# Layer 1 takes three of its blocks from SBUF, a third buffer for the norm's parts, the FFN's weights in one tile

## Chip, cores and metric

One core of a Trainium2 chip (trn2) runs the kernel. The time is that of one execution on the device, in microseconds (us). Of several executions the median is given. The engines of the core are TensorE (PE, matrix products), VectorE (DVE), ScalarE (ACT), GpSimd (POOL) and SyncE (SP, which here only issues transfers). PSUM is the memory that PE writes its sums to, SBUF the on-chip memory of all engines, DRAM the memory outside.

## What is computed

A sequence of 2048 rows with 512 features goes twice (two layers, same weights) through a state-space convolution and a gated feed-forward network, each behind a layer norm and with a residual:

```python
x = A_u                                   # [1, 2048, 512] float32
for layer in (0, 1):
    # A: causal convolution along the rows, per feature, with a kernel K of 2048 taps
    #    K[d, l] = Re(sum_n C[d, n] * exp(dt[d] * A[d, n] * l) * dt[d] * B[d, n]),  N = 128
    #    by FFT of length 4096, plus u * Dskip
    x = x + _A_ref(_layernorm(x), A_re, A_im, B_re, B_im, C_re, C_im, log_dt, Dskip)
    # B: (silu(x @ w_gate) * (x @ w_up)) @ w_down,   512 -> 1376 -> 512
    x = x + _B_ref(_layernorm(x), w_gate, w_up, w_down)
```

## The kernel before

**Blocks.** The rows are cut into four blocks of 512 (`T`). The convolution is done block by block with transforms of 1024 points: block b needs its own spectrum and those of the blocks ahead of it, each times the spectrum of a piece of K. A block is named layer.block here. Layer 1 of a block needs layer 0 of that block and of those ahead, so the order is a free choice within that: `SEQ` is 0.0, 0.1, 0.2, 1.0, 0.3, 1.1, 1.2, 1.3. The first 300 us, the front, compute K from A, B, C (`gen_tiles` makes the factors, 64 features to a chunk, eight chunks; products L509 and L510), its spectra, and split the weights of the network into a high and a low f16 part. That part's order on SP is written out by hand; elsewhere a scheduler of the language fixes each engine's order ahead of the run, from a simulated timeline and from priorities (`tc.high_priority(offset=BOOST)` lifts what is inside it). At run time every engine takes its instructions strictly in that order.

**One block of the convolution.** `inputs` (its loop prints below) loads 512 rows into the tile n, norms them (`norm_x`: twelve activations on ACT; the results of the first eight, the statistics, go to a scratch tile "junk", L223 and L225), and transforms them (`forward`: z L267, products L277 into pf, evictions such as L278). `ssm_half` does one half of the features (256): the products of spectra with vector instructions on DVE (L812, L815, 128 x 1024 each), per half four quarters with b + 1 terms; the parts w and uu are loaded from DRAM (L808, L810). Then the inverse transform (`inverse`: yl L776 on ACT, products L784 on PE into pi), and `result` adds pi to the block's residual rows xt (L232). The residual rows are the tile xs[i % 3], where i is the place of the block in `SEQ`: xs[0] and xs[1] are the halves of one tile xg, xs[2] is xf. `load_x(xt, layer, b)` fills xt ahead of `result`: for layer 0 from the input, for layer 1 from `xdr`, a DRAM tile to which each block of layer 0 is stored at the end of its network (L957, four stores of 256 KB). The tile n is loaded from the same place (L238, 1 MB), so a block of layer 1 costs two loads of 1 MB.

**One block of the network.** `ffn` works on two halves of 256 rows. `ffn_norm` norms xt: statistics on ACT (L223, L225; their results are thrown into the tile nn2), then for each of two row tiles the normed rows into nn2[:, 0] (L883), the high f16 part into half of nn2[:, 1] (L884), the low part into the other half (L885, DVE), and two DMA transposes (L887) into nh and nlo, which lie in a tile called mix. All row tiles use the same two buffers, so L884 of the next one may write only after the transpose of the one ahead has read. Gate and up products (L930, L931, L933: high x high, high x low, low x high, 256 columns) go through two PSUM buffers pgu in groups of 48; each group is followed by Silu on ACT (L936), the product on DVE (L937, both into sg), and the high and low parts hh (L938, ACT) and hl (L939, DVE). 1376 features are ten full groups of 128 and a rest of 96, which `remainder` does with the rows as the stationary side: 48 products of 96 columns in each half (L899 to L901), then L907 to L909 and four DMA transposes (L913). The down products (L946 to L948, 512 columns) end in py, which L953 adds to xt; then the store.

In the emission the convolution of the next block stands ahead of the network of this block, so that PE's products of the network run while DVE works on the next block's spectra:

```python
    for i, lb in enumerate(SEQ):
        if i + 1 < len(SEQ):
            take(ssm(*SEQ[i + 1]) if i else block1, 100)
        if i == 0:
            take(pscale, 100)
        ffn(*lb, ready if i == 0 else None)
```

## Time and profile before

| | |
|---|---|
| three runs | 1089.46, 1092.52, 1093.47 us; median 1092.52 |
| the profiled execution | 1091.58 us; from the first to the last instruction 1089.4 us |
| mean granted clock of PE | 0.986 |
| busy: PE, DVE, ACT, POOL | 1026.5 us (94%), 969.3 (89%), 547.4 (50%), 109.6 (10%) |
| moved by DMA | 149.23 MB, mean 137 GB/s |
| loads n from xdr | 4 of 1024 KB, 6.4 us from issue to landing |
| ACT from 417 us on, waiting at L223 for n | 16.1 us for xdr, 6.5 for the input |

How to read the rows: a group of instructions stands as line, engine, operation, out<-in with tile names, partitions x elements and type, x count; behind the first bar its busy us and the mean ns of one, behind the second the engine's idle time just ahead of them and what ended most of it. A row that begins with a time is a single instruction or a run of alike ones: start in us, length in us, engine, line, and in brackets the idle time ahead of it and the instruction or transfer that ended it. "PEld" is PE's loading of the stationary side, "SPq" SP's sequencer. A table by stages has one row for each stretch A:B.

### The profile page before, as it was taken

Reading aid. Unit: us, or ns where it says so; the run is one execution under the profiler, and the core shown is the slowest. Engines: PE = TensorE matmul, PEld = TensorE weight load, DVE = VectorE, ACT = ScalarE, POOL = GpSimd, SP = SyncE. Lnnn points to the kernel's source line nnn. Section 1 sums busy time; section 2 is a strip of 40 time slices with the busy share of each in tenths; the row PEclk is TensorE's granted clock in tenths of the full one; section 3 lists DMA queues with packets and bytes.
Section 4 is the critical chain, followed back from the end, with each engine's and each line's share of the span. In section 5 each row is a group of like instructions: output and inputs, shape, how many; then the busy total and the mean of one; then the engine's idle time right before and its main releaser. Section 6 shows DMA issues by size and latency. Waiting matters only on the chain.

```text
span 1089.4 us, 22811 instructions
## 1 busy us (share of the span) xinstructions
PE 1026.5 (94%) x9302; PEld 810.9 (74%) x9302; DVE 969.3 (89%) x1405; ACT 547.4 (50%) x1093; POOL 109.6 (10%) x163
## 2 busy tenths in 40 slices
PE   1989999998779999999999999999999999999998
PEld 1868888887677777686779676786867687686775
DVE  8999999998999999999999989999998999993221
ACT  6989998953367162466462253533425432134211
POOL 1112222220002010012010001201100000000000
PEclk9989999998989999999999999999999999999999
DMA  5366777768765356342444553443545245312000
GB/s 212 108 180 167 173 166 179 187 181 272 234 182 172 120 145 215 105 141 68 131 117 133 158 160 130 119 136 100 166 126 180 59 127 147 109 61 63 2 25 20
DMA packets 125003, 149.23 MB, mean 137 GB/s; under 512 B 50897, under 2 KB 75985, under 8 KB 124130
## 3 DMA queue, kind: packets, MB, share of 16 engines
q1 hardware_dynamic: 112994, 122.27, 36.8%
q0 software_dynamic: 11904, 25.50, 10.0%
q8 instruction: 73, 1.20, 0.5%
q14 instruction: 32, 0.26, 0.1%
HBM read 97.66 MB, written 33.82 MB: 121 GB/s over the span
## 4 chain that ended last, share of the span: by engine, by line
PE 27%; DVE 27%; issue 11%; DMA 5%; ACT 3%; POOL 1%; SPq 0%; DVEq 0%; POOLq 0%; ACTq 0%
PE pgu L930 5%; PE pgu L931 5%; PE pgu L933 5%; DVE t L812 4%; DVE yk L815 4%; PE py L948 3%; PE py L946 3%; PE py L947 3%; DVE yk L812 3%; PE pi L784 2%; DVE sg L937 2%; DVE hl L939 2%; DMA n<-xdr 1%; DVE yl L232 1%; DMA mix<-nn 1%
## 5 line engine op out<-in xcount | busy, mean ns | idle before, releaser
L930 PE MATMUL pgu<-mix,wsl 128*128 128x256 f16 x1280 | 298.6, 273 | 5.4 <-DVE sg L937 2.1
L931 PE MATMUL pgu<-mix,wsl 128*128 128x256 f16 x1280 | 298.4, 273 | 0.0
L933 PE MATMUL pgu<-mix,wsl 128*128 128x256 f16 x1280 | 194.8, 273 | 0.0
L931 PEld LDWEIGHTS <-wsl 128*128 128x128 f16 x1280 | 125.2, 98 | 22.5 <-issue 6.7
L933 PEld LDWEIGHTS <-wsl 128*128 128x128 f16 x1280 | 125.2, 98 | 18.4 <-issue 3.8
L930 PEld LDWEIGHTS <-wsl 128*128 128x128 f16 x1280 | 125.2, 98 | 16.4 <-issue 1.2
L946 PE MATMUL py<-wsl,hh 128*128 128x512 f16 (+1 forms) x352 | 134.2, 381 | 0.1
L948 PE MATMUL py<-wsl,hl 128*128 128x512 f16 (+1 forms) x352 | 133.5, 381 | 0.1
L947 PE MATMUL py<-wsl,hh 128*128 128x512 f16 x320 | 121.8, 381 | 0.0
L815 DVE TENSOR_TENSOR yk<-yk,t 128x1024 f32<-128x1024 f32 x96 | 116.9, 1218 | 0.5
L812 DVE TENSOR_TENSOR t<-uu,w 128x1024 f32<-128x1024 f32 x96 | 117.0, 1218 | 0.3
L938 ACT ACTIVATE hh<-sg 128x512 f16<-128x512 f32 x80 | 50.1, 627 | 114.0 <-DVE sg L937 114.0
L544 PE MATMUL pw<-kt,ek 128*128 128x256 f32 (+1 forms) x384 | 93.2, 381 | 0.0
L937 DVE SCALAR_TENSOR_TENSOR sg<-pgu,sc,sg 128x512 f32<-128x512 f32 x80 | 59.6, 745 | 37.7 <-ACT sg L936 37.6
L936 ACT ACTIVATE sg<-pgu,sc 128x512 f32<-128x512 f32 x80 | 54.2, 678 | 70.7 <-PE pgu L933 66.9
L544 PEld LDWEIGHTS pw<-kt,ek 128*128 128x128 f32 x384 | 74.8, 199 | 8.8
L939 DVE TENSOR_TENSOR hl<-sg,hh 128x512 f16<-128x512 f32 x80 | 54.8, 685 | 15.3 <-ACT hh L938 15.3
L227 POOL TENSOR_TENSOR rs<-mv,mhalf 128x2 f32<-128x2 f32 (+1 forms) x21 | 33.6, 1598 | 336.3 <-ACT mv L226 296.3
L509 PE MATMUL pk<-re,g 128*32 128x64 f32 x1024 | 65.0, 317 | 2.2 <-DMA g<-g 1.9
L948 PEld LDWEIGHTS <-hl 128*128 128x128 f16 (+1 forms) x352 | 34.4, 98 | 39.2 <-issue 0.8
L947 PEld LDWEIGHTS <-hh 128*128 128x128 f16 (+1 forms) x352 | 34.6, 98 | 38.4 <-issue 0.8
L510 PE MATMUL pk<-im,g 128*32 128x64 f32 x1024 | 63.1, 301 | 0.0
(265 smaller groups left out, 2010.1 us busy)
## 6 DMA issues: line engine op xcount, KB each, us to landing
uu<-udr SPq DMA_DIRECT2D x96, 256.0 KB, 3.0
w<-wdr SPq DMA_DIRECT2D x96, 256.0 KB, 2.8
g<-g POOLq DMA_DIRECT2D x6, 1024.0 KB, 9.2
udr<-fu POOLq DMA_DIRECT2D x22, 256.0 KB, 2.7
udr<-u SPq DMA_DIRECT2D x16, 256.0 KB, 3.3
n<-xdr SPq DMA_DIRECT2D x4, 1024.0 KB, 6.4
kdr<-ks SPq DMA_DIRECT2D x6, 512.0 KB, 2.9
kt<-kdr SPq DMA_DIRECT2D x24, 128.0 KB, 3.0
```

Of the source, the lines that this page charges most:

```text
L509: PE.matmul(o, lhsT=g[:, 0, :, d], rhs=re[:, 0:64, d], start=True, stop=False, tile_position=(0, 32 * grp))
L544: PE.matmul(pw[:, i], lhsT=e, rhs=kt[:, :, c + 4 * k0:4 * k1:4, :].rearrange("p g k d -> p k g d"), start=c == 0, stop=c == 3)
L812: V.tensor_tensor(t, uu.unsqueeze(2).to_broadcast([P, NQ, 2, 2, DC]), w.unsqueeze(3).to_broadcast([P, NQ, 2, 2, DC]), OP.mult)
L815: V.tensor_tensor(yk, yk, t, OP.add)
L930: PE.matmul(o, lhsT=wgu(wi, k, 0)[:, fs], rhs=nh[:, k], start=k == 0, stop=False)
L931: PE.matmul(o, lhsT=wgu(wi, k, 1)[:, fs], rhs=nh[:, k], start=False, stop=False)
L933: PE.matmul(o, lhsT=wgu(wi, k, 0)[:, fs], rhs=nlo[:, k], start=False, stop=k == 3)
L937: V.scalar_tensor_tensor(sg, pgu[:, 1], sc6[:, 4:5], sg, OP.mult, OP.mult)
L939: V.tensor_tensor(hl[:, f0:f0 + 2], sg, hh[:, f0:f0 + 2], OP.subtract)
L946: PE.matmul(py[r], lhsT=hh[:n, f, rc], rhs=wd(f, 0)[:n], start=f == 0, stop=False)
L947: PE.matmul(py[r], lhsT=hh[:n, f, rc], rhs=wd(f, 1)[:n], start=False, stop=False)
L948: PE.matmul(py[r], lhsT=hl[:n, f, rc], rhs=wd(f, 0)[:n], start=False, stop=f == FT - 1)
```

## The change

- **Blocks.** A table `HOME` says which buffer a block has: xs[0] for 0.0, 1.0 and 1.2, xs[1] for 0.1 and 1.1, xs[2] for 0.2, 0.3 and 1.3. So 1.0, 1.1 and 1.3 find their residual rows where layer 0 left them. For these blocks neither n nor xt is loaded; `norm_x` takes its rows from xs and writes n. Block 1.2 (`MOVED`) still goes through DRAM, in a tile `xdr` of one block, and of layer 0 only 0.2 is stored.
- **The network's norm.** The parts of a row tile take the next two of a cycle of three f16 buffers: the two halves of nn2[:, 1] and a new tile nt3. The statistics' scratch results go to nn2[:, 0] alone.
- **Weights.** The four tiles W0 to W3, in which first the factors of K and later the split weights lie, and the small tile wx become one tile `wall`; gate and up columns of one k lie at a fixed distance, so that one access covers both. `remainder` does gate and up in one product of 192 columns: 24 products in each half.

```diff
 SEQ = ((0, 0), (0, 1), (0, 2), (1, 0), (0, 3), (1, 1), (1, 2), (1, 3))
+HOME = (0, 1, 2, 0, 2, 1, 0, 2)
+MOVED = 2
...
     wmax = sb.tile([P, 2], BF16, name="wmax")
-    wx = sb.tile([P, D], F16, name="wx")
+    wall = sb.tile([P, 4, 65 * DC], F32, name="wall")
+    wflat = wall.rearrange("p t a -> p (t a)").bitcast(F16)
+    wcols = wflat[:, :16 * F].rearrange("p (w u f) -> p w u f", w=2, u=8)
     ident = sb.tile([P, P], F32, name="ident")
...
     udr = [dram.tile([NB - 1, 2, 4, P, NQ, 2, DC], F32, name=f"udr{i}") for i in range(NL)]
-    xdr = dram.tile([NB, 4, P, D], F32, name="xdr")
+    xdr = dram.tile([4, P, D], F32, name="xdr")
     kdr = dram.tile([2, 4, 32, 4, 256], F32, name="kdr")
...
+    def moved(layer, b):
+        return layer == 0 or b == MOVED
+
     def load_x(xt, layer, b):
         if layer == 0:
             nc.sync.dma_start(xt, x[0, b * T:(b + 1) * T, :].rearrange("(p c) d -> p c d", p=P))
         else:
-            nc.sync.dma_start(xt, xdr[b].rearrange("c p d -> p c d"))
+            nc.sync.dma_start(xt, xdr.rearrange("c p d -> p c d"))
...
-    def norm_x(n):
-        rs, nb = row_stats(n, 4, 1.0, "stats", lambda r: tl([P, D], "junk", "t1", BF16))
+    def norm_x(n, xt):
+        rs, nb = row_stats(xt, 4, 1.0, "stats", lambda r: tl([P, D], "junk", "t1", BF16))
         for c in range(4):
-            A.activation(n[:, c], n[:, c], AF.Identity, scale=rs[:, c:c + 1], bias=nb[:, c:c + 1])
+            A.activation(n[:, c], xt[:, c], AF.Identity, scale=rs[:, c:c + 1], bias=nb[:, c:c + 1])
...
     def gen_tiles(ch):
-        re = tl([P, 65, DC], "re", f"W{2 * (ch % 2)}")
-        im = tl([P, 65, DC], "im", f"W{2 * (ch % 2) + 1}")
+        re, im = (wall[:, 2 * (ch % 2) + i].rearrange("p (a d) -> p a d", d=DC) for i in range(2))
         mu = tl([P, 32, DC], "mu", "n")
...
     def wgu(wi, kc, lo, n=1):
-        u = 8 * wi + 4 * lo + kc
-        v = wsl[u // 6].rearrange("p (u f) -> p u f", u=6)
-        return v[:, u % 6] if n == 1 else v[:, u % 6:u % 6 + n]
+        u = 4 * lo + kc
+        return wcols[:, wi, u] if n == 1 else wcols[:, wi, u:u + n]
 
     def wd(fc, lo):
         r = 2 * fc + lo
-        if r < 5:
-            return wsl[2][:, 4 * F + r * D:4 * F + (r + 1) * D]
-        return wsl[3][:, (r - 5) * D:(r - 4) * D] if r < 21 else wx
+        return wflat[:, 16 * F + r * D:16 * F + (r + 1) * D]
...
             n = tl([P, 4, D], "n", "n")
-            load_x(n, layer, b)
-            norm_x(n)
+            xt = n if moved(layer, b) else xs[HOME[SEQ.index((layer, b))]]
+            if xt is n:
+                load_x(n, layer, b)
+            norm_x(n, xt)
             if (layer, b) == SEQ[HALF]:
...
-        xt = xs[SEQ.index((layer, b)) % 3]
+        xt = xs[HOME[SEQ.index((layer, b))]]
         ys = []
...
                 a_, b_, c_, d_ = ys
-                if h == 0 and not first:
+                if h == 0 and not first and moved(layer, b):
                     load_x(xt, layer, b)
...
         rows = TB // P
-        xt = xs[SEQ.index((layer, b)) % 3][:, s * rows:(s + 1) * rows]
+        xt = xs[HOME[SEQ.index((layer, b))]][:, s * rows:(s + 1) * rows]
         nh, nlo = nhl2[:, s % 2, 0], nhl2[:, s % 2, 1]
         with tc.high_priority(offset=BOOST):
-            rs, nb = row_stats(xt, rows, 256.0, "stats2", lambda r: nn2[:, r])
-            nt = nn2[:, 1].bitcast(F16).rearrange("p (i k) -> p i k", i=2)
+            rs, nb = row_stats(xt, rows, 256.0, "stats2", lambda r: nn2[:, 0])
             for r in range(rows):
                 A.activation(nn2[:, 0], xt[:, r], AF.Identity, scale=rs[:, r:r + 1], bias=nb[:, r:r + 1])
-                A.activation(nt[:, 0], nn2[:, 0], AF.Copy)
-                V.tensor_tensor(nt[:, 1], nn2[:, 0], nt[:, 0], OP.subtract)
+                nt = [next(parts) for _ in range(2)]
+                A.activation(nt[0], nn2[:, 0], AF.Copy)
+                V.tensor_tensor(nt[1], nn2[:, 0], nt[0], OP.subtract)
                 for i, o in enumerate((nh, nlo)):
-                    nc.sync.dma_start_transpose(o[:, :, r * P:(r + 1) * P], nt[:, i])
+                    nc.sync.dma_start_transpose(o[:, :, r * P:(r + 1) * P], nt[i])
         return nh, nlo
...
             rc = slice(r * P, (r + 1) * P)
-            for wi in range(2):
-                for k in range(4):
-                    PE.matmul(pr[:, r, wi], lhsT=nh[:, k, rc], rhs=wgu(wi, k, 0)[:, fs], start=k == 0, stop=False)
-                    PE.matmul(pr[:, r, wi], lhsT=nh[:, k, rc], rhs=wgu(wi, k, 1)[:, fs], start=False, stop=False)
-                    PE.matmul(pr[:, r, wi], lhsT=nlo[:, k, rc], rhs=wgu(wi, k, 0)[:, fs], start=False, stop=k == 3)
+            for k in range(4):
+                hi, lo = wcols[:, :, k, fs], wcols[:, :, 4 + k, fs]
+                PE.matmul(pr[:, r], lhsT=nh[:, k, rc], rhs=hi, start=k == 0, stop=False)
+                PE.matmul(pr[:, r], lhsT=nh[:, k, rc], rhs=lo, start=False, stop=False)
+                PE.matmul(pr[:, r], lhsT=nlo[:, k, rc], rhs=hi, start=False, stop=k == 3)
         with tc.high_priority(offset=BOOST):
...
                         nc.sync.dma_start(out[0, b * T:(b + 1) * T, :].rearrange("(p c) d -> c p d", c=4)[c], xt[:, r])
-                    else:
-                        nc.sync.dma_start(xdr[b, c], xt[:, r])
+                    elif moved(1, b):
+                        nc.sync.dma_start(xdr[c], xt[:, r])
...
         nn2 = tl([P, 2, D], "nn2", "nn")
+        nt3 = sb.tile([P, D], F16, name="nt3")
+        parts = itertools.cycle([nn2[:, 1].bitcast(F16)[:, i * D:(i + 1) * D] for i in range(2)] + [nt3])
     small[0] = itertools.repeat("sml")
...
```

Lines move by up to 8: L223, L225, L232, L238, L267, L776, L784, L812, L884, L899, L937, L953, L957 of before are L227, L229, L236, L245, L274, L781, L789, L817, L889, L904, L942, L958, L962 after (the load of the input, L236 before, is L243).

The order moves with it. First ACT behind the first row tiles of the network's norm in 0.2 (L883 and L884 before, L887 and L889 after), where block 1.0 is normed; yl is the inverse transform's input of the blocks around it, sg and hh the network's. Before:

```order
L883 ACTIVATE nn_3010<-xg,rs 128x512
L884 ACTIVATE nn_3010<-nn_3010 128x512
L907 ACTIVATE sg_3034<-pgu,sc_92 128x192
L909 ACTIVATE sg_3034<-sg_3034 128x2x96
L776 ACTIVATE yl_4065<-bb,sy 128x512
L936 ACTIVATE sg_3034<-pgu,sc_92 128x512
L776 ACTIVATE yl_4065<-mix,sy 128x512
L938 ACTIVATE hh<-sg_3034 128x512
L776 ACTIVATE yl_4065<-bb,sy 128x512
L936 ACTIVATE sg_3034<-pgu,sc_92 128x512
L223 ACTIVATE junk,mv<-n 128x512 x4
L776 ACTIVATE yl_4065<-bb,sy 128x512
```

After:

```order
L887 ACTIVATE nn_2990<-xg,rs 128x512
L889 ACTIVATE nn_2990<-nn_2990 128x512
L227 ACTIVATE junk,mv<-xg 128x512
L912 ACTIVATE sg_3015<-pgu,sc_92 128x192
L227 ACTIVATE junk,mv<-xg 128x512
L229 ACTIVATE junk,mv<-xg,mv 128x512 x4
L914 ACTIVATE sg_3015<-sg_3015 128x2x96
L781 ACTIVATE yl_3994<-bb,sy 128x512
L230 ACTIVATE mv<-mv,epst 128x4
L941 ACTIVATE sg_3015<-pgu,sc_92 128x512
L781 ACTIVATE yl_3994<-mix,sy 128x512
```

The statistics read xg in place of n and stand ahead of the four yl; before they stood ahead of the last one.

Second SP at the end of 0.2, whose last two stores come first in both; hh and hl are the transposes of the network's rest. Before, where xf<-xdr is the residual of 1.1 for xs[2] and n<-xdr its rows for the norm:

```order
L957 DMA xdr<-xf 128x512 x2
L238 DMA xf<-xdr 128x4x512
L808 DMA w<-wdr 128x512
L810 DMA uu<-udr_114 128x512
L913 DMA_TRANSPOSE hh<-sg_3034 128x128 x2
L913 DMA_TRANSPOSE hl<-sg_3034 128x128 x2
```

After, where xf<-in_A_u is the residual of 0.3 for xs[2]:

```order
L962 DMA xdr<-xf 128x512 x2
L813 DMA w<-wdr 128x512
L815 DMA uu<-udr_114 128x512
L918 DMA_TRANSPOSE hh<-sg_3015 128x128 x2
L918 DMA_TRANSPOSE hl<-sg_3015 128x128 x2
L243 DMA xf<-in_A_u_dram 128x2048
```

The load into xs[2] moved from ahead of the transposes to behind them, and is now that of 0.3.

Third DVE at the same place: L953 (L958 after) adds the network's output of 0.2 to its rows, and the results of the first half of 0.3 (L232 with pi before, L236 after) are written to xg before and to xf after. Before:

```order
L232 SCALAR_TENSOR_TENSOR xg<-pi,sy,xg 128x2x256
L820 TENSOR_TENSOR mix<-yk 128x256
L232 SCALAR_TENSOR_TENSOR yl_4065<-bb,sy,yl_4065 128x512
L821 TENSOR_TENSOR mix<-yk 128x256
L812 TENSOR_TENSOR t<-uu,w 128x1024
L812 TENSOR_TENSOR yk<-fu,w0r 128x1024
L953 SCALAR_TENSOR_TENSOR xf<-py,sc_92,xf 128x512 x2
L815 TENSOR_TENSOR yk<-yk,t 128x1024
L232 SCALAR_TENSOR_TENSOR xg<-pi,sy,xg 128x2x256
```

After, from the last row of 0.2 on, the last twelve rows up to the results:

```order
L817 TENSOR_TENSOR t<-uu,w 128x1024
L820 TENSOR_TENSOR yk<-yk,t 128x1024
L825 TENSOR_TENSOR bb<-yk 128x256
L826 TENSOR_TENSOR bb<-yk 128x256
L817 TENSOR_TENSOR t<-uu,w 128x1024
L772 TENSOR_TENSOR bb<-mix,bb 128x512
L942 SCALAR_TENSOR_TENSOR sg_3015<-pgu,sc_92,sg_3015 128x512
L817 TENSOR_TENSOR yk<-fu,w0r 128x1024
L773 TENSOR_TENSOR mix<-mix,bb 128x512
L944 TENSOR_TENSOR hl<-sg_3015,hh 128x512
L820 TENSOR_TENSOR yk<-yk,t 128x1024
L236 SCALAR_TENSOR_TENSOR xf<-pi,sy,xf 128x2x256 x2
```

Both results of that half now stand fifteen rows behind the last L958 of 0.2; before, one stood ahead of L953 and one two rows behind it. On PE the forward transform of 1.1's first half moved with them, from among the products of 1.0's rest to behind 135 gate and up products of 1.0.

More of the change, by code (lines that the diff above doesn't have):

```diff
@@ L83 @@
     ps = ctx.enter_context(tc.tile_pool(name="ps", bufs=1, space=PSUM))
-    BUFS = dict(W0=1, W1=1, W2=1, W3=1, ga=1, gb=1, n=1, bt=1, z=1, u=3, y1=1, uu=3, w=3, t=1, bd=2, t1=3,
+    BUFS = dict(ga=1, gb=1, n=1, bt=1, z=1, u=3, y1=1, uu=3, w=3, t=1, bd=2, t1=3,
                 xf=1, nn=1, hh=1, hl=1, sg=1, hf=1, stats=2, stats2=2, ef=1)
@@ L666, in load @@
                 st = tl([P, 4, cb], "st2", tag) if isinstance(tag, str) else \
-                    wsl[3].bitcast(F32)[:, 4 * cb * tag:4 * cb * (tag + 1)].rearrange("p (k f) -> p k f", k=4)
+                    wall[:, 3, 4 * cb * tag:4 * cb * (tag + 1)].rearrange("p (k f) -> p k f", k=4)
                 nc.sync.dma_start(st, src[:, fs].rearrange("(k p) f -> p k f", p=P))
@@ L917, in ffn @@
             rows = TB // P
-            xt = xs[SEQ.index((layer, b)) % 3][:, s * rows:(s + 1) * rows]
+            xt = xs[HOME[SEQ.index((layer, b))]][:, s * rows:(s + 1) * rows]
             nh, nlo = ready if ready and s == 0 else ffn_norm(layer, b, s)
@@ L1159 @@
                 f()
-        wsl = []
         loads, his, los = split_weights()
@@ L1174 @@
         xs[0], xs[1] = xg[:, 0], xg[:, 1]
-        wsl += [tl([P, 6 * F], f"wsl{k}", f"W{k}", F16) for k in range(4)]
         load_x(xs[0], 0, 0)
```

## The prediction

> **What bounds the kernel now.** I read the page first (busy shares and slices), then the table by stages, then the rows of TensorE (PE) with idle time ahead of them, then what ScalarE (ACT) did at those moments. Blocks are named layer.block.
>
> The page, and the table by stages from the first product of FFN 0.1 on; each stretch runs to the first product of the next FFN. Columns: length, then busy us of PE, weight loads, DVE, ACT, POOL, the granted PE clock, the DMA share, GB/s.
>
> ```profile
> span 1089.4 us, 22811 instructions
> 417.50:520.60 103.10, 100.56 (x850) 77.35 (x847) 99.83 (x159) 55.55 (x113) 10.82 (x14) 1.00 0.40 127
> 520.60:619.50 98.90, 96.80 (x802) 73.14 (x800) 95.81 (x138) 43.57 (x84) 3.29 (x5) 0.98 0.43 130
> 619.50:718.40 98.90, 95.54 (x802) 72.92 (x800) 95.09 (x140) 43.56 (x85) 10.92 (x13) 1.00 0.46 139
> 718.40:813.50 95.10, 94.97 (x802) 72.76 (x800) 94.39 (x140) 33.92 (x63) 7.69 (x12) 1.00 0.44 132
> 813.50:911.90 98.40, 94.05 (x786) 70.93 (x784) 90.08 (x127) 40.89 (x81) 4.43 (x5) 1.00 0.46 131
> 1002.10:1085.50 83.40, 83.10 (x664) 61.83 (x661) 18.46 (x29) 14.74 (x24) 0.20 (x1) 1.00 0.07 22
> ```
>
> From 417 us to the end PE is the bound: it is all but never idle, and the last 83 us are its products alone. VectorE (DVE) is nearly as full until 912. So time goes only where PE gets fewer products or fewer stalls. These are PE's rows behind the larger stalls; in brackets the idle time and what ended it:
>
> ```profile
> 436.30 0.27 PE L784 MATMUL pi<-yl,mix 128*128 128x256 f16 x1 [1.41 <-ACT yl L776]
> 476.53 0.27 PE L784 MATMUL pi<-yl,mix 128*128 128x256 f16 x1 [0.99 <-ACT yl L776]
> 539.33 0.27 PE L784 MATMUL pi<-yl,mix 128*128 128x256 f16 x1 [2.02 <-ACT yl L776]
> 633.14 0.27 PE L930 MATMUL pgu<-mix,wsl 128*128 128x256 f16 x1 [1.64 <-DVE sg L937]
> 665.30 0.27 PE L784 MATMUL pi<-yl,mix 128*128 128x256 f16 x1 [1.40 <-ACT yl L776]
> 832.44 0.27 PE L930 MATMUL pgu<-mix,wsl 128*128 128x256 f16 x1 [0.45 <-DVE sg L937]
> 837.63 0.38 PE L277 MATMUL pf<-z,eh 128*128 128x256 f16 x2 [0.99 <-ACT z L267]
> 868.32 0.38 PE L277 MATMUL pf<-z,eh 128*128 128x256 f16 x2 [2.50 <-ACT fbt L278]
> ```
>
> Eight stalls, 11.40 us. The page counts a 256-column product as 0.27 us though the next starts 0.11 later (rows below), so each stall is 0.16 us longer than its bracket: 12.7 us in all, the ceiling of what fewer waits can give here. Now ACT, which takes its queue in order:
>
> ```profile
> 433.08 0.63 ACT L223 ACTIVATE junk<-n 128x512 bf16<-128x512 f32 x1 [2.74 <-DMA n<-xdr]
> 473.92 0.63 ACT L223 ACTIVATE junk<-n 128x512 bf16<-128x512 f32 x1 [6.46 <-DMA n<-in_A_u_dram]
> 536.14 0.63 ACT L223 ACTIVATE junk<-n 128x512 bf16<-128x512 f32 x1 [3.51 <-DMA n<-xdr]
> 638.30 0.63 ACT L223 ACTIVATE junk<-n 128x512 bf16<-128x512 f32 x1 [4.55 <-DMA n<-xdr]
> 825.03 0.63 ACT L223 ACTIVATE junk<-n 128x512 bf16<-128x512 f32 x1 [5.30 <-DMA n<-xdr]
> 867.15 0.63 ACT L884 ACTIVATE nn<-nn 128x512 f16<-128x512 f32 x1 [2.81 <-DMA mix<-nn]
> ```
>
> At 433, 536 and 825 ACT stands before the norm of 1.0, 1.1 and 1.3 until its load has landed; behind it in the queue are the conversions (yl L776, z L267) and the Silu work that PE waits for at 436, 539, 832 and 837. At 867 ACT waits for a transpose to leave the norm's buffer, and the eviction L278 behind it frees PE at 868. PE's stalls are ACT's waits for DMA, passed on.
>
> **Part by part.** *Three blocks stay in SBUF.* The loads of n and of xt for 1.0, 1.1 and 1.3 go, and 12 of 16 stores. No engine works less: the norm's twelve activations read xs in place of n. What goes is the wait, and the new order starts the statistics as rows come out of the FFN. Counted at the stalls: 1.0: 1.41 + 0.16 = 1.57. 1.1: 2.02 + 0.16 = 2.18, and a stretch at half clock after it:
>
> ```profile
> 536.00:540.00 4.00, 1.99 (x17) 1.44 (x16) 3.29 (x6) 3.86 (x11) 0.00 (x0) 1.00 0.41 122
> 540.00:543.40 3.40, 3.40 (x10) 1.20 (x9) 2.70 (x4) 3.40 (x10) 0.00 (x0) 0.50 0.04 13
> ```
>
> 3.40 us at 0.50 cost 1.7 us, and I count them to the stall ahead of them, where PE was busy for 1.99 of 4.00 us. (The Trainium skill, "TensorE: Matmul & The Clock Gate", section "What's actually happening", asks for a whole idle window of some 3.4 us before the clock halves; by it the 1.7 us would not belong to this stall. The row shows the drop behind a shorter one.) 1.3: 0.45 + 0.99 + 2 x 0.16 = 1.76. Sum: 7.2 us. It is no more than that, since what each norm is worth is its PE stall and not ACT's whole wait; it could be 0 if ACT's next queue entry were late at the same place. The order speaks against that for 1.0 and 1.1: the statistics stand ahead of the first yl and wait only for rows that DVE wrote before. 1.2 still goes through DRAM, and 0.3 still loads the input: their waits of 4.55 and 6.46 us stay.
>
> *Third buffer for norm parts.* Each row tile takes the next two of three buffers (1 KB a partition each), so the second tile's copy (L884 before) need not wait for the first one's transpose; the statistics no longer write over both. Its worth is the stall at 868: 2.50 + 0.16 = 2.7 us. The second tile's remainder (L885) now waits for the first tile's first transpose, on DVE; behind it stand FFN outputs and products. That transpose is issued one step earlier than the one that ACT waited for, so I take 0, at most the 2.81 us seen on ACT, which would put the 2.7 back.
>
> *Last features in one product.* 24 in place of 48 products a half-block, of 192 columns in place of 96, 16 half-blocks: 768 become 384. Rows from the last block, where PE waits for nothing, and two six-packs from the front, one with contiguous moving data (L309), one with runs of 16 elements (L544):
>
> ```profile
> 1000.06 0.21 PE L899 MATMUL pgu<-wsl,mix 128*128 128x96 f16 x1
> 1002.10 0.27 PE L930 MATMUL pgu<-mix,wsl 128*128 128x256 f16 x1
> 1005.60 0.60 PE L933 MATMUL pgu<-mix,wsl 128*128 128x256 f16 x4
> 1006.91 0.60 PE L933 MATMUL pgu<-mix,wsl 128*128 128x256 f16 x4
> 99.70 1.46 PE L309 MATMUL pf<-n,ek 128*128 128x256 f32 x6
> 103.74 1.46 PE L544 MATMUL pw<-kt,ek 128*128 128x256 f32 x6
> L899 PEld LDWEIGHTS <-mix 128*128 128x128 f16 x256 | 25.0, 98 | 3.7 <-issue 1.5
> ```
>
> From 1000.06 to 1002.10 are 48 products of 96 columns: 42.5 ns each. From 1005.60 to 1006.91 are 12 of 256: 109.2 ns. The line through both is 2.5 ns + 0.417 ns a column: 82.5 ns at 192. So 768 x 42.5 = 32.6 us becomes 384 x 82.5 = 31.7: 1.0 us less, 0 if a product's cost went with its columns alone. Two runs of 96 instead of one cost nothing extra by the equal rows at 99.70 and 103.74. (The Trainium skill, the same page, section "Back-to-back issue gap", gives pairs of weight load and product in a real kernel as some 81 ns at 128 columns and 131 at 512. A straight line through these makes 77 and 89 ns, an estimate, and 59.0 - 34.3 = 24.7 us less. The trace disagrees: its pairs follow each other in 42.5 ns.)
>
> *One tile for the weights.* The same bytes in another arrangement. The order of the front is the same on every engine up to FFN 0.0, so its 300 us stay.
>
> *Input of 0.3 into xs[2].* Here a wait comes in. Block 0.2 lies there, so the load has to follow the two last stores of 0.2, and in the new SP order it also stands behind four transposes:
>
> ```profile
> 617.67 0.98 SPq L957 DMA_DIRECT2D xdr<-xf  x2
> 620.76 0.37 SPq L238 DMA_DIRECT2D xf<-xdr  x1
> 622.62 2.41 SPq L913 DMA_TRANSPOSE hh<-sg  x2
> 625.13 3.61 SPq L913 DMA_TRANSPOSE hl<-sg  x2
> 630.88 0.38 SPq L238 DMA_DIRECT2D n<-xdr  x1
> L812 DVE TENSOR_TENSOR t<-uu,w 128x1024 f32<-128x1024 f32 x96 | 117.0, 1218 | 0.3
> ```
>
> Before, the load into this buffer (for 1.1) left at 620.76. Now it is issued between then and 628.7 (625.13 + 3.61), and landed 7.4 us later like the load of n (630.88 to ACT's 638.30): 628.2 to 636.1. DVE reaches the two result steps of 0.3 fifteen instructions after the last output of 0.2 (store at 617.67 + 0.66): six of 1.22 us, nine of 0.35 to 0.75, some 11.7 us, so at 630. It waits 0 to 6.1 us, I take 2.5. Behind them stand the Silu product (L937) that frees PE's next buffer and the evictions of forward 1.1, which holds PE back by less: it has 135 products of 109 ns (14.7 us, to about 634) ahead of that forward in its order. I put 1 us on PE.
>
> *Given back.* PE that stalls less reaches DVE's results earlier, and from 520 to 814 DVE is busy for 285.3 of 292.9 us: at 633 and 665 PE already waited for late DVE work (1.64, 1.40). I put 2 us for waits that turn up so; bounds 0 and the 7.2 us of the norms.
>
> Sum: -7.2 - 2.7 - 1.0 + 1 + 2 = -7.9 us. The profiled execution took 1091.58 us (span 1089.4 and 2.2 around it), 0.94 under the median of three runs, 1092.52; from it 1083.7, from the median 1084.6. I say **1084**.
>
> **Rivals.** Half a per cent of this kernel, 5.5 us, is about what a measurement of it can tell from no change.
>
> *A: the stalls only move.* DVE is as full as PE, so stalls that ACT caused come back as stalls for DVE. For it: the DVE shares above, and that 633 and 665 have nothing to do with loads. Against it: DVE itself lost 8.3 us between 813.5 and 911.9, mostly while ACT stood still, and gets that back too; and each PE stall read above is an ACT wait for DMA. Only the product and the transposes would count: 1091.6 - 3.7, 1087 to 1092.
>
> *B: the load of 0.3 becomes the bound, slower.* DVE stands before the result steps, both buffers of the inverse's sums stay held, and forward 1.1, which the new order puts 14.7 us later, comes too late for DVE. With 6.1 us of waiting and 14.7 of delay unhidden: 1091.6 - 10.9 + 20.8 = 1101.5. It decides only from where the forward's delay exceeds the products of 0.3's second half; that half alone has 4 x 7 vector steps of 1.22 us, 34 us, so it should be hidden.
>
> *C: weight loads set the pace of the small products.* At 98 ns a load (row above), 384 fewer would save 37.6 us: 1054. The page's rule above is of this kind. Against it: loads overlap, 48 pairs took 2.04 us.
>
> *D: one tile is treated as one object,* and each chunk's factors, which now lie in parts of it, wait in the front for the products of the chunk before.
>
> ```profile
> L509 PE MATMUL pk<-re,g 128*32 128x64 f32 x1024 | 65.0, 317 | 2.2 <-DMA g<-g 1.9
> ```
>
> These are the products of eight chunks on the real factors alone: 65.0 / 8 = 8.1 us a chunk, and with seven chunks that wait 57 us, so some 1148. Against it: the front's order and waits do not change.
>
> **The numbers.** Forecast 0.58 (1079 to 1087); more of the twelve microseconds goes and nothing returns, 0.07 (1075 to 1079); A 0.23; B 0.08; C 0.02; D 0.02. Faster by over 0.5% (under 1087.1): 0.58 + 0.07 + 0.02 = 0.67. Within: 0.23. Slower: 0.10. The range takes in the forecast, A to its end at 1092, and the upside but for its last microsecond: 1076 to 1092, 0.86 or so.
>
> **What would show it.** Right: no ACT row "junk" waiting for n<-xdr but one; ACT's copy of norm parts without a DMA wait near 868; the small products 82 ns apart; PE's stalls from 417 on down from 12.7 to about 5 us plus no half clock near 540. Wrong: DVE idle before the results of 0.3 for over 6 us; a product of 192 columns at 85 ns or more; new idle rows of PE before L784 that end on DVE; or the first product of FFN 0.1 later than 417.

## The result

| | before | changed |
|---|---|---|
| runs of this comparison | 1089.46 to 1093.47, median 1092.72 us | 1075.85, 1076.04, 1077.30 us |
| ratio of the times | | 0.9859, 95% interval 0.9835 to 0.9882 |
| profiled execution, its span | 1091.58, 1089.4 us | 1077.30, 1075.0 us |
| moved by DMA | 149.23 MB | 139.74 MB |
| first product of FFN 0.1 | 417.5 us | 415.4 us |
| from there to the last output: products alone | 650.6 us | 649.8 us |
| from there to the last output: PE's stalls | 17.1 us | 5.1 us |

The changed kernel is 15.4 us faster (1092.72 x 0.0141; by the interval 13 to 18; the two medians lie 16.7 us apart). A fourth execution, with a granted clock of 0.846, is left out, and so is one each, at 0.658 and 0.562, of two later runs.

The last two lines are worked out from the trace: each product's start is taken from the next one's, the pitch of its kind (the time from one start to the next where nothing waits: 42.5, 82.5, 109.2 or 215.9 ns for 96, 192, 256 and 512 columns) is taken off, and what is left over 20 ns counts as a stall; what half clock costs is in it. So of the 14.4 us between the two spans, 12.0 are stalls of PE, 0.8 products, and 2.1 were won ahead of FFN 0.1; 0.5 were lost behind the last product.

The table by stages of the changed kernel, with the columns of before; the stages are FFN 0.1, 0.2, 1.0, 0.3 and 1.1:

```profile
span 1075.0 us, 22004 instructions
415.40:516.50 101.10, 100.16 (x802) 77.37 (x800) 100.28 (x160) 56.80 (x116) 10.79 (x14) 1.00 0.32 94
516.50:609.80 93.30, 93.30 (x740) 71.38 (x738) 92.54 (x134) 40.89 (x76) 3.45 (x5) 1.00 0.38 105
609.80:705.00 95.20, 94.46 (x749) 72.25 (x747) 92.79 (x138) 43.33 (x85) 10.62 (x13) 1.00 0.47 147
705.00:803.60 98.60, 96.95 (x769) 74.22 (x767) 95.97 (x143) 36.58 (x68) 6.85 (x12) 1.00 0.39 121
803.60:897.20 93.60, 92.98 (x736) 70.97 (x734) 92.73 (x131) 39.95 (x77) 4.60 (x5) 1.00 0.41 115
```

FFN 0.2, in which 1.1 is normed, goes from 98.90 to 93.30 us with no idle time left. FFN 0.3 is longer than before (98.60 to 95.10): products moved into it, and three of the six stalls that are left stand there. All of them, on PE:

```profile
469.44 0.27 PE L935 MATMUL pgu<-mix,wall 128*128 128x256 f16 x1 [0.94 <-DVE sg L913]
655.79 0.27 PE L789 MATMUL pi<-yl,mix 128*128 128x256 f16 x1 [0.74 <-ACT yl L781]
754.77 0.82 PE L284 MATMUL pf<-z,eh 128*128 128x256 f16 x6 [0.60 <-ACT fbt L285]
768.42 0.27 PE L935 MATMUL pgu<-mix,wall 128*128 128x256 f16 x1 [0.55 <-DVE sg L942]
774.75 0.27 PE L935 MATMUL pgu<-mix,wall 128*128 128x256 f16 x1 [0.50 <-DVE sg L942]
809.67 0.27 PE L935 MATMUL pgu<-mix,wall 128*128 128x256 f16 x1 [0.62 <-DVE sg L913]
```

The longest bracket is 0.94 us, and four of six end on DVE. On ACT the statistics (first row: those that read a loaded n; second and third: those that read rows left in SBUF), and the copies of the norm's parts; on DVE the remainders:

```profile
L227 ACT ACTIVATE junk<-n 128x512 bf16<-128x512 f32 x8 | 4.9, 618 | 3.2 <-DMA n<-xdr 2.5 <-DMA n<-in_A_u_dram 0.7
L227 ACT ACTIVATE junk<-xg 128x512 bf16<-128x512 f32 x6 | 3.8, 626 | 14.4 <-DVE xg L958 14.4
L227 ACT ACTIVATE junk<-xf 128x512 bf16<-128x512 f32 x4 | 2.5, 628 | 8.6 <-DVE xf L958 8.6
L889 ACT ACTIVATE nn<-nn 128x512 f16<-128x512 f32 x16 | 10.0, 624 | 0.3
L890 DVE TENSOR_TENSOR nn<-nn 128x512 f16<-128x512 f32 x8 | 5.5, 689 | 0.9 <-DMA mix<-nn 0.9
L890 DVE TENSOR_TENSOR nt<-nn 128x512 f16<-128x512 f32 x8 | 5.5, 688 | 1.8 <-DMA mix<-nt 1.8
```

ACT's waits for loads went from 16.1 + 6.5 us to 2.5 + 0.7, its wait for transposes is gone, and DVE now waits 2.7 us for transposes. ACT does not stand less ahead of its statistics, though: for 23.0 us it now waits there for DVE's L958, which writes the rows. What changed is where it stands: none of the six stalls ends on an ACT row right behind one of these waits.

### The profile page after: what moved, and what is told of

It reads as the page before. It is cut to its first block, busy times and chain, and to the rows that moved or that the text cites. A ratio compares the mean times of both kernels' runs of the same rounds, so it can differ in the third digit from the quotient of the medians.

```text
span 1075.0 us, 22004 instructions
## 1 busy us (share of the span) xinstructions
PE 1015.1 (94%) x8918; PEld 801.8 (75%) x8918; DVE 966.5 (90%) x1405; ACT 544.4 (51%) x1093; POOL 103.9 (10%) x163
## 2 busy tenths in 40 slices
DMA packets 120104, 139.74 MB, mean 130 GB/s; under 512 B 50609, under 2 KB 75697, under 8 KB 119234
## 4 chain that ended last, share of the span: by engine, by line
DVE 37%; PE 27%; issue 4%; DMA 3%; ACT 3%; POOL 1%; DVEq 0%; SPq 0%; ACTq 0%; POOLq 0%
DVE t L817 5%; PE pgu L938 5%; PE pgu L935 5%; PE pgu L936 5%; DVE yk L820 5%; DVE yk L817 4%; PE py L951 3%; PE py L952 3%; PE py L953 3%; DVE sg L942 2%; DVE yl L236 2%; DVE hl L944 2%; DMA st<-in_B_w_down_dram 1%; PE pi L789 1%; PE pw L550 1%
## 5 line engine op out<-in xcount | busy, mean ns | idle before, releaser
L935 PE MATMUL pgu<-mix,wall 128*128 128x256 f16 x1280 | 299.0, 273 | 5.8 <-DVE sy L629 2.1
L936 PE MATMUL pgu<-mix,wall 128*128 128x256 f16 x1280 | 298.9, 273 | 0.0
L938 PE MATMUL pgu<-mix,wall 128*128 128x256 f16 x1280 | 195.7, 273 | 0.0
L936 PEld LDWEIGHTS <-wall 128*128 128x128 f16 x1280 | 125.2, 98 | 22.6 <-issue 7.0
L935 PEld LDWEIGHTS <-wall 128*128 128x128 f16 x1280 | 125.2, 98 | 16.4 <-issue 0.9
L938 PEld LDWEIGHTS <-wall 128*128 128x128 f16 x1280 | 125.2, 98 | 14.6
L951 PE MATMUL py<-wall,hh 128*128 128x512 f16 (+1 forms) x352 | 133.4, 379 | 0.0
L952 PE MATMUL py<-wall,hh 128*128 128x512 f16 (+1 forms) x352 | 133.4, 379 | 0.0
L953 PE MATMUL py<-wall,hl 128*128 128x512 f16 (+1 forms) x352 | 132.2, 379 | 0.0
L817 DVE TENSOR_TENSOR t<-uu,w 128x1024 f32<-128x1024 f32 x96 | 117.5, 1224 | 0.2
L942 DVE SCALAR_TENSOR_TENSOR sg<-pgu,sc,sg 128x512 f32<-128x512 f32 x80 | 60.0, 750 | 39.2 <-ACT sg L941 39.2
L953 PEld LDWEIGHTS <-hl 128*128 128x128 f16 (+1 forms) x352 | 34.3, 98 | 38.0
L952 PEld LDWEIGHTS <-hh 128*128 128x128 f16 (+1 forms) x352 | 34.4, 98 | 37.7
L951 PEld LDWEIGHTS <-hh 128*128 128x128 f16 (+1 forms) x352 | 34.4, 98 | 37.3
L515 PE MATMUL pk<-wall,g 128*32 128x64 f32 x1024 | 57.4, 288 | 4.9 <-DMA g<-g 3.7
L516 PE MATMUL pk<-wall,g 128*32 128x64 f32 x1024 | 57.8, 287 | 0.7 <-issue 0.7
```

The costliest lines, as they stand in the source:

```text
L516: PE.matmul(o, lhsT=g[:, 1, :, d], rhs=im[:, 0:64, d], start=False, stop=True, tile_position=(0, 32 * grp))
L817: V.tensor_tensor(t, uu.unsqueeze(2).to_broadcast([P, NQ, 2, 2, DC]), w.unsqueeze(3).to_broadcast([P, NQ, 2, 2, DC]), OP.mult)
L935: PE.matmul(o, lhsT=wgu(wi, k, 0)[:, fs], rhs=nh[:, k], start=k == 0, stop=False)
L936: PE.matmul(o, lhsT=wgu(wi, k, 1)[:, fs], rhs=nh[:, k], start=False, stop=False)
L938: PE.matmul(o, lhsT=wgu(wi, k, 0)[:, fs], rhs=nlo[:, k], start=False, stop=k == 3)
L942: V.scalar_tensor_tensor(sg, pgu[:, 1], sc6[:, 4:5], sg, OP.mult, OP.mult)
```

## The experiments

The theory ahead of the runs: the time is won where ACT no longer waits for the load of n; the other parts are worth about what the prediction gave them. The rivals: the traffic that went counts, not the wait; or the other parts and the front hold what the prediction's terms don't explain.

"Changed" is the kernel with all parts, 1076.0 us (the middle of its three runs). Each run's ratio is to the kernel before on the same chip, whose medians were 1091.7 to 1092.9; so a difference between two kernels that did not run side by side carries about 1 us of that.

**Blocks through DRAM again.** All else as changed:

```diff
-HOME = (0, 1, 2, 0, 2, 1, 0, 2)
+HOME = (0, 1, 2, 0, 1, 2, 0, 1)
 def moved(layer, b):
-    return layer == 0 or b == MOVED
+    return True
```

with four blocks in `xdr`.

> The changed kernel with its first part undone: all layer-1 blocks go through DRAM again, the third norm buffer and the wide product stay. Theory (most of the gain is this part: the norms' own stalls, 7.2 us, and those that came with them at the norm of 0.3 and behind it, about 4 us): 1076 + 11, so about 1087, with ACT waiting for n<-xdr some 16 us again and PE's stalls behind 417 us back at 12 to 15 us. Rival (this part is worth only the 7.2 us that the prediction priced, and the rest of the 16 us comes from the other parts or from the front): about 1083.

1085.96 us, 0.9937 (0.9917 to 0.9957): 9.9 us over changed, 14.2 us of stalls, as the theory had it. But ACT waits for n from xdr 11.4 us and not some 16, and the stalls are other ones than before, as will be seen.

**Blocks alone.** The kernel before with `HOME`, `moved` and `norm_x(n, xt)`, and nothing else.

> The kernel before with the first part alone: three blocks stay in SBUF; two buffers for the norm's parts, products of 96 columns and the old weight tiles stay. Theory: 1092.5 - 11, so about 1081.5, with the stall of 2.5 us behind the copy of the norm's parts still there. Rival (worth 7.2 us): about 1085.

1083.48 us, 0.9924 (0.9903 to 0.9944): 8.4 us, between the two. 8.3 us of stalls are left, the largest 1.66; the stall of 2.5 us behind the copy, which the theory kept, is not among them, though ACT's copies (L891 here) still wait 8.0 us for transposes.

**Two buffers for the norm's parts.**

```diff
-    rs, nb = row_stats(xt, rows, 256.0, "stats2", lambda r: nn2[:, 0])
+    rs, nb = row_stats(xt, rows, 256.0, "stats2", lambda r: nn2[:, r])
+    nt = nn2[:, 1].bitcast(F16).rearrange("p (i k) -> p i k", i=2)
     for r in range(rows):
...
-        nt = [next(parts) for _ in range(2)]
```

> The changed kernel with two buffers for the norm's parts again. Theory (the third buffer is worth the one stall of 2.7 us at 868 in the trace of before): 1076 + 2.7, about 1079, with ACT waiting for a transpose at the copy. Rival A (with the norms out of the way that stall is hidden or elsewhere): 1076. Rival B (all the gain that the norms do not explain is here): 1080 or more.

1080.13 us, 0.9891 (0.9871 to 0.9911): 4.1 us over changed. ACT waits for transposes again, at the copy and at the first statistic behind it:

```profile
L889 ACT ACTIVATE nn<-nn 128x512 f16<-128x512 f32 x24 | 15.0, 627 | 8.9 <-DMA mix<-nn 8.5
L227 ACT ACTIVATE nn<-xg 128x512 f32<-128x512 f32 x12 | 7.5, 626 | 17.2 <-DMA mix<-nn 8.3 <-DVE xg L236 5.0 <-DVE nn L890 4.0
```

The stalls (8.9 us) are not one of 2.7 but thirteen of up to 1.4; rival B's size came, not its reason.

**Products of 96 columns** out of the one tile: the loop over `wi` of before, in `remainder`.

> The changed kernel with the last features in products of 96 columns again, out of the one weight tile. Theory (2.5 ns of fixed cost a product, 384 more products): 1076 + 1.0, about 1077. Rival (each product costs its weight load too): 1076 + 37.6, about 1114. Rival (the narrow products also held up Silu work behind them): 1078 to 1080.

1076.11 us, 0.9850 (0.9829 to 0.9871): no difference from changed. Its products alone take 650.6 us, those of changed 649.8, and its stalls 4.9 in place of 5.1; 0.8 us is less than the runs can tell. The rivals with weight loads or Silu work are out.

**Norm from DRAM, residual rows in SBUF.** All of layer 0 is stored and n is loaded in each block of layer 1; xt is not:

```diff
-            xt = n if moved(layer, b) else xs[HOME[SEQ.index((layer, b))]]
-            if xt is n:
-                load_x(n, layer, b)
-            norm_x(n, xt)
+            load_x(n, layer, b)
+            norm_x(n, n)
...
-                    elif moved(1, b):
-                        nc.sync.dma_start(xdr[c], xt[:, r])
+                    else:
+                        nc.sync.dma_start(xdr[b, c], xt[:, r])
```

> The changed kernel, where the three blocks keep their residual rows in SBUF (no xt load), but the norm reads its rows through DRAM again: all of layer 0 is stored, n is loaded for 1.0, 1.1 and 1.3. Theory (what counts is that ACT's queue waits for the load of n): most of the 10 us that undoing the whole part cost comes back, so 1084 to 1086, with ACT at L227 waiting for n<-xdr some 16 us. Rival (the loads of xt and the share of the DMA engines count as much): about half, 1080 to 1082.

1084.29 us, 0.9933 (0.9918 to 0.9948): 8.3 of the 9.9 us come back with the load of n, as the theory had it. ACT waits 10.1 us for n from xdr (not 16) and 8.9 for the input.

**Stores back.** Only the second part of that diff.

> The changed kernel with the 12 stores of layer 0's other three blocks back (3 MB of the 9.5 MB that went), read by nobody. Theory (waits count, not traffic): 1075 to 1077. Rival (traffic counts; a third of the 10 us): about 1079.

1074.86 us, 0.9849 (0.9831 to 0.9867): 12 stores more cost nothing. The 3 MB are not what was saved. The run before this one has the same stores and differs from it by the three loads of n alone: they cost 9.4 us, side by side. That this is the wait and not the 3 MB of these loads is argued: the three loads of xt, as large, cost some 1.7 us (1085.96 against 1084.29, not side by side).

**Block 1.0 alone through DRAM.**

```diff
-    return layer == 0 or b == MOVED
+    return layer == 0 or b in (0, MOVED)
```

> The changed kernel with block 1.0 alone going through DRAM again (stored, n and xt loaded). Theory (one tile n serves all norms, so a late norm of 1.0 also makes the load for 0.3 late): the load of n for 0.3 is issued near 467 us again in place of 450, ACT waits for it by 4 us or more, and both norms' PE stalls return, 1.6 + 1.2 us, so about 1079. Rival (only the norm's own stall returns): 1077.6, and the load for 0.3 stays near 450.

1081.64 us, 0.9911 (0.9892 to 0.9930): 5.6 us for one block of three. When SP issues the load of n for 0.3, in the kernel before, in changed and here:

```profile
467.65 0.33 SPq L236 DMA_DIRECT2D n<-in_A_u_dram  x1
```

```profile
450.41 0.33 SPq L243 DMA_DIRECT2D n<-in_A_u_dram  x1
```

```profile
465.10 0.33 SPq L243 DMA_DIRECT2D n<-in_A_u_dram  x1
```

What follows from it here, on ACT and on PE:

```profile
473.13 0.63 ACT L227 ACTIVATE junk<-n 128x512 bf16<-128x512 f32 x1 [8.32 <-DMA n<-in_A_u_dram]
...
478.54 0.71 ACT L781 ACTIVATE yl<-mix,sy 128x512 f16<-128x512 f32 x1
```

```profile
434.47 0.27 PE L789 MATMUL pi<-yl,mix 128*128 128x256 f16 x1 [1.84 <-ACT yl L781]
479.29 0.35 PE L789 MATMUL pi<-yl,mix 128*128 128x256 f16 x1 [3.59 <-ACT yl L781]
```

One tile n serves every norm. A late norm of 1.0 holds it 15 us longer, the load for 0.3 leaves 15 us later, and PE stands at the norm of 0.3 too, longer (3.59 + 0.16 us, and 3.4 us at half clock) than at the norm of 1.0. The chain is the theory's, its price twice what the text above gave it.

**The load of 1.2 in four parts,** one `dma_start(xt[:, c], xdr[c])` for each row tile.

> The changed kernel with the loads of block 1.2 split into four of 256 KB, so that the norm's statistics can begin with the first row tile. Theory (ACT's last wait for n<-xdr, 2.5 us, shrinks, and the PE stall of 0.9 us at 656 with it): 1075 to 1076. Rival (that stall is DVE's, the wait is beside it): 1076 to 1077.

1075.61 us, 0.9854 (0.9833 to 0.9875), as changed. ACT's first statistic began at 641.08 in place of 642.70, but the order had put it ahead of a Silu and a copy that stood before it, so that ACT waited longer (7.16 us) with these behind it; the stall at 656 stayed (1.18 us, 0.91 in changed). The rival: the yl that PE waits for there had itself waited for DVE's bb, 1.82 us in changed and 1.87 here.

**The one tile alone:** changed with the edits of the first, third and fourth experiment together. The second text is that of one more execution, of which the profile is shown.

> The changed kernel with all parts undone but the one weight tile: blocks through DRAM, two buffers for the norm's parts, products of 96 columns. Theory (the tile is another arrangement of the same bytes): 1092, within 2 us of before, first product of FFN 0.1 at 417 to 419. Rival (the front gains some 3 us from the tile, since the first product of FFN 0.1 was at 417.5 and 418.7 in the two kernels with the old tiles and at 413.6 to 416.9 in the eight with the new one): 1089, that product near 415.

> The kernel with the one tile alone once more, for an undisturbed profile; it took 1089.6 us, and with the third buffer added 1080.3. Theory (the buffer's 9 us are only in part its own waits; the rest is that the two orders differ): some 16 us of stalls on PE from 417 us on; those that end on ACT's copy or on work behind its wait for a transpose sum to 3 to 5 us, the other 4 to 6 us stand at norms and DVE work at which the kernel with the buffer has a different order on ACT. Rival (all 9 us are waits for the norm's buffers): ACT and DVE wait for mix<-nn ahead of stalls of 8 us or more.

1089.26 us, 0.9976 (0.9962 to 0.9991): 1 to 4 us faster than before; the one further execution took 1087.75 us and has the first product of FFN 0.1 at 414.1. The rival of the first text: the tile has a gain of its own. The second text is answered below the table of versions.

**The kernel before, again.**

> The kernel before, profiled a second time, to see how far one execution's front differs from another's. Theory (the 2.1 us that the changed kernel was ahead at the first product of FFN 0.1 are the spread of the front): that product between 415 and 418.7. Rival (it is a property of the kernel): within 0.5 us of 417.5. The stalls of PE behind it should be the eight of the first profile, 17 us in all, in either case.

One execution, 1091.03 us: that product at 417.3, 16.7 us of stalls, the same eight large ones. So it is not the spread of the front. In three profiles with the old tiles it stands at 417.3 to 418.7, in ten with the one tile at 413.6 to 416.9. Where it may come from can be seen in the factors' products of the last chunk, in the kernel before (second profile) and with the one tile alone:

```profile
248.55 0.49 PE L509 MATMUL pk<-re,g 128*32 128x64 f32 x8
248.84 0.44 PE L510 MATMUL pk<-im,g 128*32 128x64 f32 x8
249.08 0.50 PE L509 MATMUL pk<-re,g 128*32 128x64 f32 x8
...
251.12 0.51 PE L509 MATMUL pk<-re,g 128*32 128x64 f32 x8
```

```profile
246.46 0.45 PE L515 MATMUL pk<-wall,g 128*32 128x64 f32 x8
246.69 0.44 PE L516 MATMUL pk<-wall,g 128*32 128x64 f32 x8
246.91 0.45 PE L515 MATMUL pk<-wall,g 128*32 128x64 f32 x8
...
248.67 0.46 PE L515 MATMUL pk<-wall,g 128*32 128x64 f32 x8
```

From the first row to the last are 80 products: 2.57 us and 2.21, so 32 and 28 ns each. A whole chunk of 256 takes 8.1 us with the old tiles and mostly 7.0 with the new one, some 8 us over eight chunks. From 50 to 250 us DVE is the busier engine (195.8 of 200 us, PE 193.7), so that not all of it shows in the time: at DVE's row beside the last chunk the kernel with the one tile is 2.1 us ahead, and 1.1 of that is a shorter wait of DVE:

```profile
249.62 0.96 DVE L572 TENSOR_TENSOR wo<-pw,wo 128x768 f32<-128x768 f32 x1 [1.25 <-ACT w0r L568]
```

```profile
247.49 0.96 DVE L578 TENSOR_TENSOR wo<-pw,wo 128x768 f32<-128x768 f32 x1 [0.17 <-ACT w0r L574]
```

That the faster products are the cause of the 2 to 3 us at FFN 0.1 is argued from these rows; the two kernels differ in nothing but the tile.

**Tile and third buffer,** blocks through DRAM, 96 columns: the edits of the first and the fourth experiment.

> The kernel with the one tile and the third buffer for the norm's parts; blocks through DRAM and products of 96 columns as before. Theory (the third buffer is worth 3 to 4 us here too, the wide product under 1): 3 to 4 us under the kernel with the one tile alone, and 0 to 1 over the one that has the wide product as well (1086.0), so 1086 to 1088. Rival (the third buffer pays only when the norms do not wait): as the kernel with the one tile alone, some 1091.

1080.31 us, 0.9897 (0.9876 to 0.9918). Here the theory fell. This kernel differs from the first experiment's by the narrow products alone, which cost 0.8 us more of PE, and it is 5.6 us *faster* (4.4 by the ratios). It waits longer for loads, 18.7 + 6.1 us on ACT against 11.4 + 8.3, and has 7.5 us of stalls against 14.2. At the norm of 0.3, first with the wide products, then with the narrow ones:

```profile
472.97 0.63 ACT L227 ACTIVATE junk<-n 128x512 bf16<-128x512 f32 x1 [8.28 <-DMA n<-in_A_u_dram]
...
478.37 0.71 ACT L781 ACTIVATE yl<-mix,sy 128x512 f16<-128x512 f32 x1
```

```profile
471.42 0.63 ACT L227 ACTIVATE junk<-n 128x512 bf16<-128x512 f32 x1 [6.11 <-DMA n<-in_A_u_dram]
...
473.27 0.70 ACT L781 ACTIVATE yl<-mix,sy 128x512 f16<-128x512 f32 x1
```

```profile
479.13 0.37 PE L789 MATMUL pi<-yl,mix 128*128 128x256 f16 x1 [3.55 <-ACT yl L781]
```

```profile
474.03 0.27 PE L789 MATMUL pi<-yl,mix 128*128 128x256 f16 x1 [0.65 <-ACT yl L781]
```

ACT stands before the same load in both. But with the wide products the scheduler put seven statistics, a Silu and a short copy ahead of the first yl (5.4 us behind the landing), with the narrow ones three (1.85 us). The order of a few rows on ACT decides whether the wait reaches PE.

All versions side by side; 1 says that a part is in, "front" is the first product of FFN 0.1, products and stalls are from there on:

| tile | third buffer | blocks | wide | us | front | products | stalls |
|---|---|---|---|---|---|---|---|
| 0 | 0 | 0 | 0 | 1092.7 | 417.5 | 650.6 | 17.1 |
| 0 | 0 | 1 | 0 | 1083.5 | 418.7 | 650.6 | 8.3 |
| 1 | 0 | 0 | 0 | 1089.3 | 414.1 | 650.6 | 16.7 |
| 1 | 1 | 0 | 0 | 1080.3 | 415.8 | 650.6 | 7.5 |
| 1 | 1 | 0 | 1 | 1086.0 | 415.7 | 649.8 | 14.2 |
| 1 | 0 | 1 | 1 | 1080.1 | 416.9 | 649.8 | 8.9 |
| 1 | 1 | 1 | 0 | 1076.1 | 414.1 | 650.6 | 4.9 |
| 1 | 1 | 1 | 1 | 1076.0 | 415.4 | 649.8 | 5.1 |

The products are 650.6 us in all with narrow ones and 649.8 in all with wide ones; front and stalls make the time. The parts don't add up. The blocks are worth 8.4 us alone (against the runs beside them), 9.9 on top of all else with the wide products, 4.2 with the narrow ones; the third buffer 9.0 without the blocks and 4.1 with them; the wide product nothing, or 5.6 us to the bad. Blocks and third buffer take away stalls of the same kind, ACT waiting for a DMA with PE's work behind it. With the tile alone ACT waits for the norm's transposes by 9.2 + 7.4 + 0.7 us:

```profile
L889 ACT ACTIVATE nn<-nn 128x512 f16<-128x512 f32 x24 | 15.0, 625 | 9.4 <-DMA mix<-nn 9.2
L227 ACT ACTIVATE nn<-xg 128x512 f32<-128x512 f32 x16 | 10.0, 625 | 11.5 <-DMA mix<-nn 7.4 <-DVE xg L236 2.3 <-DVE nn L890 1.8
L227 ACT ACTIVATE nn<-xf 128x512 f32<-128x512 f32 x8 | 5.0, 623 | 6.4 <-DVE nn L890 3.5 <-DVE xf L236 2.1 <-DMA mix<-nn 0.7
```

One of these waits reaches PE: the copy at 861.66 waits, the eviction behind it comes late, and PE's forward transform with it:

```profile
861.66 0.63 ACT L889 ACTIVATE nn<-nn 128x512 f16<-128x512 f32 x1 [3.16 <-DMA mix<-nn]
862.20 0.58 ACT L285 ACTIVATE fbt<-pf 128x512 f32<-128x512 f32 x1
```

```profile
862.83 0.27 PE L284 MATMUL pf<-z,eh 128*128 128x256 f16 x1 [2.86 <-ACT fbt L285]
```

Behind it come 3.4 us at half clock; stall and half clock make 4.7 of the 9.2 us of stalls between the two kernels, within the 3 to 5 of the second text. The four other stalls over 1 us of that kernel stand at norms and DVE work: 1.97, 1.10 and 2.28 at yl, 2.76 at DVE's sg. At the same products the kernel with the buffer has, in its order, 0.95 and 0.65, then 0.37 and 0.24 around the third and none at the fourth; 1.14 and 0.64, at DVE's sg, stand one and two groups of products away from these. Whether that is the buffer or the order that came with it no run tells. No version here is faster than changed by more than the measurement can tell.

## Why the prediction was right

**The forecast and the time.** Direction and mechanism were right, the size was not: the sum gave -7.9 us, and 15.4 came. The 1076.04 us lie at the very end of the stated 1076 to 1092, outside the 1079 to 1087 that the forecast stood for, in the 1075 to 1079 that had a chance of 0.07. That the range held is luck: its lower end stands for the case in which more of the twelve microseconds goes and nothing comes back, but 3.4 us of stalls did come in other places, and 2.1 us were won in the front, for which no term stood. Part by part of the 14.4 us between the profiled spans: the sum had 6.9 us fewer stalls, and there were 12.0; 1.0 of products, 0.8; nothing in the front, 2.1; nothing behind the last product, where 0.5 were lost.

**The bound.** It held: from 417 us on the time is PE's products, 650 to 651 us in every version, and its stalls. Its ceiling of 12.7 us was too low: with the 1.7 at half clock and 2.7 in stalls of under 0.5 us there were 17.1. The prediction looked for the gain at PE's stalls and for nothing in the traffic; the stores put back bear out the latter for their 3 MB.

**Norms, -7.2 us.** The mechanism was right: the stalls at 436, 539, 832 and 837 and the half clock at 540 are gone, and with the load of n most of the time comes back. The size was too small. "1.2 still goes through DRAM, and 0.3 still loads the input: their waits of 4.55 and 6.46 us stay" is the step that failed: they shrank to 2.5 and 0.7. The load of 0.3 waits for the tile n, which 1.0 now leaves 17 us earlier (issued at 450.41, before at 467.65). The stall at 476 (0.99 + 0.16 us) went with it. That at 633 (1.80) is gone and that at 665 (1.56) shrank to 0.91; the prediction had left both in place. At 633 PE waited for DVE's sg (L937), and between the last output of 0.2 and that sg DVE had five rows of 1.1's forward transform, 4.0 us; in the new order none stands there. That this is why the stall went is a reading of the two orders, which no run isolates.

**Third buffer, -2.7.** 4.1 us on top of the rest. The 868 stall was the one place where the wait reached PE in the order of before; with the tile alone ACT's waits for transposes were 17.3 us, and in other orders they come out elsewhere. DVE's new wait (2.7 us, bound 2.81) cost PE nothing that shows.

**Wide product, -1.0.** 0.8 us fewer products, pitch 82.5 ns as worked out, but its time is within the noise, and in one setting the new order that came with it cost 5.6 us more than it saved.

**One tile, 0.** Failed: "The order of the front is the same on every engine up to FFN 0.0, so its 300 us stay". The order is the same, but the factors' products got from 32 to 28 ns, and FFN 0.1 began 2 to 3 us earlier. Rival D looked at this place and for the opposite sign.

**Input of 0.3, +1.** The load left at 617.73, behind the transposes as foreseen, but landed 5.0 us later and not 7.4, and DVE waited for it 0.23 us, PE not at all:

```profile
622.72 1.41 DVE L236 SCALAR_TENSOR_TENSOR xf<-pi,sy,xf 128x512 f32<-128x512 f32 x2 [0.23 <-DMA xf<-in_A_u_dram]
```

**Given back, +2.** Of the six stalls that are left (5.0 us with their 0.16 each) three are new and two, at 469 and 755, grew from 0.3: 3.4 us in place of the 2 given. The prediction's sign of about 5 us of stalls left came true, but by luck: both what there was to go (17.1 in place of 12.7 + 1.7) and what came were larger.

Rival A (stalls only move) is refuted for this order: 17.1 to 5.1. The argument against it was wrong in part: not every PE stall was an ACT wait for DMA. The row at 633 ends on DVE, and the yl behind the one at 665 had waited 7.12 us for DVE. And the first experiment, with 14.2 us of stalls at other places, shows that a new order can do just that. Rivals B, C and D did not come.

## What to carry to other kernels

A wait on an engine beside the bound is worth what the bound's engine waits behind it, and that hangs on the few rows that stand between the wait and the work that is needed: read the order there, and count on the parts of a change not adding up when a scheduler lays the rows anew for each. When a norm comes earlier, follow its tile: what is loaded into it next also comes earlier. An edit that moves tiles can change the rate of products that read them; compare the pitch of the same products before and after, not only their order.

## What the runs showed of the hardware

A short stall can be paid for twice, once as idle time and once as half clock behind it. In the kernel with narrow products, the stall at 655 us and the stretches around it:

```profile
655.14 0.32 PE L789 MATMUL pi<-yl,mix 128*128 128x256 f16 x1 [2.20 <-ACT yl L781]
```

```profile
651.80:655.20 3.40, 1.20 (x26) 1.09 (x25) 3.40 (x5) 1.47 (x3) 0.00 (x0) 1.00 0.51 154
655.20:658.60 3.40, 3.40 (x30) 2.89 (x30) 3.40 (x7) 1.14 (x2) 0.00 (x0) 0.50 0.11 40
```

PE was busy for 1.20 of 3.40 us, and the next 3.40 ran at half clock (products of 96 columns followed each other in 80 ns there, not 42.5): 1.7 us of work lost behind a stall of 2.20 + 0.16. In other kernels stalls of 2.9 us and more were followed by 3.4 us at half clock or 6.8; of those between 2.1 and 2.7, some were: in the two profiles of the kernel before, the stall at 539 was (2.18 with its 0.16) and was not (2.14), the one at 866 to 868 was not (2.67) and was (2.48). (The Trainium skill, "TensorE: Matmul & The Clock Gate", section "What's actually happening", asks for at least one idle window of about 3.4 us; the row above shows a busy share of a third in 3.40 us, so the trace does not agree.)

The factors' products, 64 columns of f32 at a stride of 256 bytes, take 32 ns each out of the four tiles and mostly 28 out of the one, the same reads otherwise. Whether that is the place in SBUF or something else was not tried.
